# Loading the first chunks of wq in sets of every 4th or 2nd row, one row a descriptor

## The chip, the cores and the metric

The kernel runs on one core of a Trainium2 chip. The metric is the time of one execution on the device, in microseconds (us). The profile's span, from the first to the last instruction, is about 1.8 us shorter. The PE (TensorE) clock is granted in steps; the profile lists the granted share. Six runs of the kernel before on one chip lay within 0.3 us.

## The reference, cut to what matters

A decode step for one token: layer norm, attention over the last 4096 keys of 32 heads, output projection, and a gated MLP. Only the first product matters for the change.

```python
q = (x @ wq).reshape(B, Sq, Hq, Dh)          # x: 1 x 640, wq: 640 x 6144, bfloat16
k = k_cache[:, :, Sk - W:, :]                # 32 heads x 4096 keys x 192
v = v_cache[:, :, Sk - W:, :]
p = softmax(einsum(q, k) * Dh ** -0.5);  o = einsum(p, v)
h = x + o.reshape(1, 1, Hq * Dh) @ wo        # then the MLP on h
```

wq is 7.9 MB, k and v together 101 MB. Everything is read once.

## The kernel before

wq comes in five chunks of 128 rows by 6144 columns (1536 KB in the units of the profile). Two chunks share one large buffer. `load` puts one DMA on the queue of the sync engine (SP). The list of loads is `wq, k0, k1, k2, v0, ...`, and SP issues them in order, as far as buffers and semaphores allow.

```python
wq_v = A_wq.rearrange("(c p i) n -> c p (i n)", c=DC, i=4)   # 32 groups of 4 rows: 49152 contiguous bytes
...
def dma_wq(i):
    t = kvp.tile([P, KVE], BF16, tag="kv", name="wq_t")
    for c in range(2 * i, min(2 * i + 2, DC)):
        load(t[:, (c % 2) * HD:(c % 2 + 1) * HD], wq_v[c])   # one load: 128 partitions of 12288 bytes
    tiles[("wq", i)] = t
...
# q = x @ wq: six groups of matmuls; the first one takes chunk after chunk as it lands
for c in range(DC):
    for a in range(2):
        nc.tensor.matmul(psv, lhsT=xn2[:, c, a, :], rhs=wc[:, gq:gq + 4, a, w0:w0 + P], ...)
...
# the last v load, and the product with the last part of wo
nc.tensor.matmul(pv[p0:p0 + 2, 0:Dh], lhsT=E[:, j, :], rhs=vt[:, j * Dh:(j + 1) * Dh], ...)
nc.tensor.matmul(attn_ps[:, nb:nb + 1], lhsT=wo_t[:, ...], rhs=o[:, i:i + 1], ...)
```

The loads use eight semaphores in turn. The ninth load in flight has to wait until the first has landed. Three tiny loads from ScalarE's queue (x and two scalars) take part in the turn.

## Time and profile before

| | before |
|---|---|
| time, median (range) | 286.71 us (286.56 to 286.80, 6 runs) |
| span of the profiled run | 284.7 us |
| first load issued / first packets start | 0.74 / about 2.1 us |
| last wq chunk landed | 21.95 us |

From the page of the kernel before: span, busy time, the DMA row in 40 slices (tenths) with its GB/s, the load queue (packets, MB, share of 16 engines' span) and the shares of the chain that ended last.

```profile
span 284.7 us, 3101 instructions
PE 167.1 (59%) x1110; PEld 65.3 (23%) x1110; DVE 218.4 (77%) x288; ACT 75.2 (26%) x380; POOL 2.3 (1%) x10
...
DMA  8999999999998999999999999999999999999993
GB/s 332 435 435 408 435 429 402 444 463 435 435 435 382 435 442 443 427 464 424 414 442 421 443 428 439 407 457 428 410 435 456 442 442 383 435 435 425 401 406 141
...
q1 hardware_dynamic: 5384, 119.35, 97.8%
...
DMA 42%; DVE 41%; PE 13%; issue 2%; SPq 1%; ACT 0%; DVEq 0%; ACTq 0%
```

The load queue keeps 16 engines busy for 97.8% of the span. No compute engine comes near that. The chain's 41% for DVE is a trap: those links end in loads that already lie in a long queue (the k loads land 29.8 us after their issue, in the median).

The table of stretches shows it by stage. Its columns are the stretch, then busy time of PE, weight loads, DVE, ACT and POOL, the granted PE clock, the DMA share and GB/s.

```profile
core 0: us, PE busy (x) PEld busy (x) DVE busy (x) ACT busy (x) POOL busy (x), PEclk, DMA share, GB/s
2.00:22.00 20.00, 5.00 (x16) 1.78 (x17) 6.75 (x48) 0.22 (x2) 0.95 (x1) 1.00 1.03 433
220.00:274.00 54.00, 37.30 (x343) 16.36 (x342) 39.41 (x58) 6.72 (x24) 0.00 (x0) 0.90 0.99 421
```

A DMA share of 1.03 and 0.99, and 1.00 or 1.01 in the stretches between them: the stream is never empty until the tail. (A transfer is credited to the stretch in which it starts, so a share can pass 1.)

The timeline of the start shows SP's issues and the first matmuls of q. The columns are start, duration, engine, line, operation, operands, count, and in brackets the idle time before and what ended it.

```profile
0.74 3.15 SPq L58 DMA_DIRECT2D wq_t<-in_A_wq_dram  x5
...
9.76 1.03 PE L264 MATMUL sc_ps<-wq_t,xn_126 128*128 128x512 bf16 x2 [2.25 <-DVE xn_126 L251]
...
11.03 1.01 PE L264 MATMUL sc_ps<-wq_t,xn_126 128*128 128x512 bf16 x2 [0.24 <-DMA wq_t<-in_A_wq_dram]
...
14.70 1.01 PE L264 MATMUL sc_ps<-wq_t,xn_126 128*128 128x512 bf16 x2 [2.66 <-DMA wq_t<-in_A_wq_dram]
...
18.34 1.01 PE L264 MATMUL sc_ps<-wq_t,xn_126 128*128 128x512 bf16 x2 [2.63 <-DMA wq_t<-in_A_wq_dram]
...
21.95 2.29 PE L264 MATMUL sc_ps<-wq_t,xn_126 128*128 128x512 bf16 x5 [2.60 <-DMA wq_t<-in_A_wq_dram]
```

Each chunk lands about 3.65 us after the one before (11.03, 14.70, 18.34, 21.95). The first matmul at 9.76 waits for x, not for wq. So the landing of the last chunk tells how late the stream is.

Some readings need the packet records of the trace. Each holds start, duration, size and queue of one packet, but not its engine. A packet of 49152 B normally takes 1.815 us, one of 12288 B 0.460 us. Below, "excess" is what packets last beyond that, summed and divided by 16 engines. "Delay of the stream" is the mean end of the last 1024 packets of 49152 B (k and v), against the same packets of the kernel before.

### The profile page before, as it was taken

Reading aid. Unit: us, or ns where it says so; the run is one execution under the profiler, and the core shown is the slowest. Engines: PE = TensorE matmul, PEld = TensorE weight load, DVE = VectorE, ACT = ScalarE, POOL = GpSimd, SP = SyncE. Lnnn points to the kernel's source line nnn. Section 1 sums busy time; section 2 is a strip of 40 time slices with the busy share of each in tenths; the row PEclk is TensorE's granted clock in tenths of the full one; section 3 lists DMA queues with packets and bytes.
Section 4 is the critical chain, followed back from the end, with each engine's and each line's share of the span. In section 5 each row is a group of like instructions: output and inputs, shape, how many; then the busy total and the mean of one; then the engine's idle time right before and its main releaser. Section 6 shows DMA issues by size and latency. Waiting matters only on the chain.

```text
span 284.7 us, 3101 instructions
## 1 busy us (share of the span) xinstructions
PE 167.1 (59%) x1110; PEld 65.3 (23%) x1110; DVE 218.4 (77%) x288; ACT 75.2 (26%) x380; POOL 2.3 (1%) x10
## 2 busy tenths in 40 slices
PE   0329935773755377725852585536971767764774
PEld 0103412221211022211220121112320222321463
DVE  7300099889999999998499999996699949995443
ACT  2001247413274431122344440143101010202301
POOL 3000000000000000000000000000000000000000
PEclk9999979796598557955799558955797797999785
DMA  8999999999998999999999999999999999999993
GB/s 332 435 435 408 435 429 402 444 463 435 435 435 382 435 442 443 427 464 424 414 442 421 443 428 439 407 457 428 410 435 456 442 442 383 435 435 425 401 406 141
DMA packets 5404, 119.53 MB, mean 420 GB/s; under 512 B 973, under 2 KB 2254, under 8 KB 2830
## 3 DMA queue, kind: packets, MB, share of 16 engines
q1 hardware_dynamic: 5384, 119.35, 97.8%
q8 instruction: 8, 0.13, 0.2%
q14 instruction: 6, 0.05, 0.0%
q10 hardware_dynamic: 6, 0.00, 0.0%
HBM read 119.34 MB, written 0.00 MB: 419 GB/s over the span
## 4 chain that ended last, share of the span: by engine, by line
DMA 42%; DVE 41%; PE 13%; issue 2%; SPq 1%; ACT 0%; DVEq 0%; ACTq 0%
DVE k_t L316 22%; DMA k_t<-in_A_k_cache_dram 21%; DMA v_t<-in_A_v_cache_dram 9%; DMA wq_t<-in_A_wq_dram 7%; DMA wo_t<-in_A_wo_dram 5%; PE sc_ps L264 5%; DVE S L309 5%; DVE ob L437 4%; DVE S L330 4%; PE sc_ps L323 3%; PE pv_174 L412 1%; PE attn_ps L473 1%; SPq L58 1%; PE sm_ps L340 1%; DVE gm L342 1%
## 5 line engine op out<-in xcount | busy, mean ns | idle before, releaser
L316 DVE TENSOR_TENSOR k_t<-k_t,q_205 128x6144 bf16<-128x6144 bf16 x32 | 107.1, 3351 | 13.1 <-DMA k_t<-in_A_k_cache_dram 13.1
L323 PE MATMUL sc_ps<-k_t,ident_bf 128*128 128x512 bf16 x282 | 87.1, 468 | 50.6 <-DVE k_t L316 50.6
L306 ACT ACTIVATE k_t<-k_t 128x192 bf16<-128x192 bf16 x144 | 49.9, 347 | 32.8 <-DVE k_t L316 32.8
L323 PEld LDWEIGHTS <-ident_bf 128*128 128x128 bf16 x282 | 30.6, 113 | 98.3 <-issue 63.9
L306 ACT ACTIVATION_READ_ACCUMULATOR k_t<-k_t 128x1 f32 x144 | 26.8, 186 | 0.0
L309 DVE TENSOR_REDUCE S<-k_t 128x16 f32<-128x3072 bf16 x8 | 26.8, 3345 | 0.0
L264 PE MATMUL sc_ps<-wq_t,xn_126 128*128 128x512 bf16 x60 | 17.4, 449 | 10.4 <-DMA wq_t<-in_A_wq_dram 8.1
L330 DVE TENSOR_REDUCE S<-sc_ps 128x16 f32<-128x512 f32 (+1 forms) x32 | 21.8, 682 | 0.5 <-PE sc_ps L323 0.5
L273 DVE TENSOR_SCALAR sp_f<-sm_ps 128x1 f32<-128x1 f32 x3 | 0.3, 153 | 25.3 <-PE sm_ps L270 25.3
L359 ACT ACTIVATE E_125<-S,bias 128x64 bf16<-128x64 f32 x10 | 3.5, 360 | 48.1 <-DVE bias L349 48.1
L359 ACT ACTIVATE E_123<-S,bias 128x64 bf16<-128x64 f32 x12 | 4.2, 360 | 41.9 <-DVE bias L349 41.9
L359 ACT ACTIVATE E_124<-S,bias 128x64 bf16<-128x64 f32 x10 | 3.5, 361 | 37.9 <-DVE bias L349 37.9
L266 ACT ACTIVATE q_205<-sc_ps 128x512 bf16<-128x512 f32 x6 | 3.6, 597 | 30.1 <-PE sc_ps L264 30.1
L264 PEld LDWEIGHTS <-xn_126 128*128 128x128 bf16 x60 | 6.5, 109 | 20.9 <-issue 13.6
L412 PE MATMUL pv_174<-v_t,E_124 128*8 128x512 bf16 (+1 forms) x72 | 8.9, 521 | 2.0 <-DMA v_t<-in_A_v_cache_dram 2.0
L342 DVE TENSOR_REDUCE gm<-sm_ps 2x1 f32<-2x128 f32 x16 | 4.5, 278 | 7.1 <-PE sm_ps L340 7.1
L412 PE MATMUL pv_172<-v_t,E_125 128*8 128x512 bf16 (+1 forms) x72 | 7.5, 472 | 3.1 <-DMA v_t<-in_A_v_cache_dram 3.1
L412 PE MATMUL pv_174<-v_t,E_123 128*8 128x512 bf16 (+1 forms) x48 | 5.8, 521 | 1.0 <-DMA v_t<-in_A_v_cache_dram 1.0
L412 PE MATMUL pv_172<-v_t,E_123 128*8 128x512 bf16 (+1 forms) x72 | 6.2, 424 | 0.0
L412 PE MATMUL pv_174<-v_t,E_125 128*8 128x512 bf16 (+1 forms) x48 | 5.0, 474 | 1.6 <-DMA v_t<-in_A_v_cache_dram 1.6
L412 PEld LDWEIGHTS <-E_125 128*8 128x8 bf16 (+1 forms) x120 | 3.5, 87 | 9.3 <-issue 7.2
L412 PEld LDWEIGHTS <-E_124 128*8 128x8 bf16 (+1 forms) x120 | 3.6, 89 | 8.3 <-issue 6.4
(237 smaller groups left out, 148.3 us busy)
## 6 DMA issues: line engine op xcount, KB each, us to landing
k_t<-in_A_k_cache_dram SPq DMA_DIRECT2D x15, 3072.0 KB, 29.8
v_t<-in_A_v_cache_dram SPq DMA_DIRECT2D x15, 3072.0 KB, 29.6
wq_t<-in_A_wq_dram SPq DMA_DIRECT2D x5, 1536.0 KB, 11.2
wo_t<-in_A_wo_dram SPq DMA_DIRECT2D x7, 960.0 KB, 19.9
k_t<-in_A_k_cache_dram SPq DMA_DIRECT2D x2, 1536.0 KB
v_t<-in_A_v_cache_dram SPq DMA_DIRECT2D x1, 1536.0 KB
w_in_sb<-in_B_w_in_dram SPq DMA_DIRECT2D x2, 576.0 KB, 14.6
wo_t<-in_A_wo_dram SPq DMA_DIRECT2D x2, 480.0 KB, 13.8
```

What stands on the lines that cost most here:

```text
L58: eng.add_instruction(mybir.InstDMACopy(name=nc.get_next_instruction_name(), mode="Copy", queue="qSPDynamicHW", ins=eng.lower_ap_dma(in_, ...
L264: nc.tensor.matmul(psv, lhsT=xn2[:, c, a, :], rhs=wc[:, gq:gq + 4, a, w0:w0 + P], start=(c == 0 and a == 0), stop=(c == DC - 1 and a == 1))
L266: nc.scalar.activation(out=q2f[:, gq:gq + 4, w0:w0 + P], in_=psv, func=ACT.Copy, scale=scale / 16)
L306: nc.scalar.activation(out=k3[:, j, :], in_=k3[:, j, :], func=ACT.Copy, accum_out=S[:, j:j + 1])
L309: nc.vector.tensor_reduce(out=st[t]["S"][:, J - JS:J], in_=products(t)[:, J - JS:J, :], axis=AX.X, op=ALU.add)
L316: nc.vector.tensor_tensor(out=kc, in0=kc, in1=q2[:, t:t + 1, :].to_broadcast([P, JC, Dh]), op=ALU.mult)
L323: nc.tensor.matmul(psv, lhsT=ident_bf[:], rhs=products(t)[:, j0:j1, n * g:(n + 1) * g], start=(n == 0), stop=(n == Dh // g - 1))
L330: nc.vector.tensor_reduce(out=S[:, j0:j1], in_=st[t]["ps"][ch], axis=AX.X, op=ALU.add)
L342: nc.vector.tensor_reduce(out=gm[:], in_=mT[0:2, 0:P], axis=AX.X, op=ALU.max)
L359: nc.scalar.activation(out=E[:, :, a], in_=S[:], func=ACT.Exp, bias=bias[:, a:a + 1], accum_out=zq[q][:, a, b:b + 1])
L412: nc.tensor.matmul(pv[p0:p0 + 2 * n, :].rearrange("p (k r i) -> p k r i", k=n, r=32), lhsT=E[:, j0:j0 + n, :].rearrange("p j a -> p (j a)" ...
L437: nc.vector.tensor_reduce(out=ob[:, i0:i0 + ni], in_=flat.rearrange("p (k r i) -> p i r k", k=n, i=ni), axis=AX.X, op=ALU.add)
```

## The change

The intent, as far as the code tells it: smaller first loads with fewer descriptors, so that the stream starts sooner, each row on its own partition, in sets spread over all partitions. The first two chunks come in 4 sets of 32 rows, the next two in 2 sets of 64 rows, the last as before.

```diff
+    wq_rows = A_wq.rearrange("(c p) n -> c p n", c=DC)
+    WQ_PARTS = (4, 4, 2, 2, 1)
...
         for c in range(2 * i, min(2 * i + 2, DC)):
-            load(t[:, (c % 2) * HD:(c % 2 + 1) * HD], wq_v[c])
+            n = WQ_PARTS[c]
+            for j in range(n):
+                dst = t[j::n, (c % 2) * HD:(c % 2 + 1) * HD]
+                load(dst, wq_rows[c, j::n] if n > 1 else wq_v[c])
```

## The prediction

> **What bounds the kernel now.** The input stream. The page puts the load queue at 97.8% of 16 engines' span; the table of stretches shows a DMA share of 0.99 to 1.03 in every stretch from 2 to 274 us, while DVE has 77% and PE 59% of the span. By the packet records the 16 engines together lack only about 0.6 us of work between the first 5 us and the last 5. The chain of waits names DMA 42% and DVE 41%, but its DVE links end in loads that lie 14 to 30 us in the queue; a wait on DVE only shortens that backlog. Time = start of the stream + packet time per engine + about 10 us of tail after the last wo landing (274.0). The change can only act on the first two.
>
> **What it changes.** PE, DVE, ACT and POOL keep their instructions. On SP, four wq loads of 1536 KB become 4, 4, 2 and 2 loads, 13 in place of 5, the same bytes. Each of 16 engines moves such a chunk as 8 packets of 12288 B instead of 2 of 49152 B. The Trainium skill ("DMA: Bandwidth & Descriptors", Why a DMA increments its semaphore by 16 and not by 1) takes the largest count up to 16 that divides both slowest dimensions, so 32 and 64 rows still give 16 engines; the trace agrees for 32 source rows (2 packets on each engine). Eight more loads are a whole turn of the eight load semaphores, so later loads keep theirs.
>
> **Costs.** Packet records: 49152 B take 1.815 us, 12288 B (a late v load) 0.461. Four chunks: 32 x 0.461 - 8 x 1.815 = +0.23 us per engine. Eight more semaphore writes of about 0.01: at most +0.1. SP takes 0.55 to 0.63 us per load; a set of 32 rows lasts 0.92 on the engines, so SP keeps ahead. From the sixth load on SP waits for an earlier landing (reused semaphores), but with about 3.6 us of work queued, so I expect no hole.
>
> **Gains.** SP issues the first load at 0.74 us, packets start near 2.1, on five engines only at 2.7 to 2.9: 0.27 us idle per mean engine. The first 16 packets last on average 0.57 us more than 1.815. I read both as descriptors for 128 destination rows being made while engines wait; with 32 rows there are a quarter of them. At most 0.84 us (estimate) is to be had; I expect 0.65 of it.
>
> **On the critical path:** all of it, as the stream is never empty later: -0.65 + 0.3 = -0.35 us, 0.1%. Predicted 286.2 us, 8 in 10 within 285.5 to 286.8. Faster by over 2%: 0.005; within 2%: 0.985; slower by over 2%: 0.01.
>
> **What would show it right.** All engines start by about 2.2 us and the first packets last under 0.6 us; the wait for the last wq landing (21.95 us before, chain of waits) ends at 21.3 to 21.8; the last wo landing is earlier by as much; PE, DVE and ACT busy times stay; about 384 more data packets. The first wq matmul (9.76) waits for xn2, so PE starts no earlier.
>
> **What would make it wrong.** The 0.57 us is first access to memory and stays: then +0.1 to +0.3. A hole between sets because a short load is made slower than it is moved (DMA share below 1 in 3 to 8 us): up to +1. Strided single rows slower than 0.461. Or the queue runs dry later where I do not see it.

## The result

| | before | changed |
|---|---|---|
| time, median (range), 6 runs each | 286.71 us (286.56 to 286.80) | 288.25 us (287.92 to 289.31) |
| ratio, 95% interval | | 1.0059 (1.0041 to 1.0076) |
| span, profiled run | 284.7 | 286.8 |
| last wq chunk landed | 21.95 us | 22.90 us |
| delay of the stream | | 0.94 us |

A ratio is the mean time of one kernel's fast runs over that of the other's of the same rounds, so it is not quite the ratio of the medians. Executions over 1.5% slower than the fastest of the same kernel are left out of the means. The change is clear of noise, within 2%, and slower. It was predicted slightly faster, and the range (285.5 to 286.8) does not hold it.

The same lines of the page of the changed kernel, without the chain:

```profile
span 286.8 us, 3115 instructions
PE 169.8 (59%) x1110; PEld 66.2 (23%) x1110; DVE 218.2 (76%) x288; ACT 75.2 (26%) x380; POOL 2.3 (1%) x10
...
DMA  7999999999999999999999999999999999999991
GB/s 257 396 451 439 432 440 440 441 418 432 425 439 427 425 439 433 414 477 421 425 425 446 419 415 439 451 447 439 427 402 442 425 432 410 470 439 398 396 407 73
...
q1 hardware_dynamic: 5896, 119.35, 97.4%
```

PE, DVE and ACT do the same work. What differs is the first slice or two of the GB/s row: 257 and 396 instead of 332 and 435. The timeline of the start of the changed kernel:

```profile
0.74 8.46 SPq L58 DMA_DIRECT2D wq_t<-in_A_wq_dram  x13
...
9.75 1.04 PE L269 MATMUL sc_ps<-wq_t,xn_134 128*128 128x512 bf16 x2 [2.25 <-DVE xn_134 L256]
...
11.89 1.01 PE L269 MATMUL sc_ps<-wq_t,xn_134 128*128 128x512 bf16 x2 [1.10 <-DMA wq_t<-in_A_wq_dram]
...
19.26 1.03 PE L269 MATMUL sc_ps<-wq_t,xn_134 128*128 128x512 bf16 x2 [2.61 <-DMA wq_t<-in_A_wq_dram]
...
22.90 5.42 PE L269 MATMUL sc_ps<-wq_t,xn_134 128*128 128x512 bf16 x14 [2.60 <-DMA wq_t<-in_A_wq_dram]
```

The first matmuls that wait for a chunk, the second one, already come late (11.89 instead of 11.03). From then on the distance between chunks is about as before (19.26 to 22.90, 3.64 us), so nearly all of the loss is at the start. The last chunk is 0.95 us late.

The table of stretches for 5 to 12 us, first of the kernel before, then of the changed kernel:

```profile
core 0: us, PE busy (x) PEld busy (x) DVE busy (x) ACT busy (x) POOL busy (x), PEclk, DMA share, GB/s
5.00:8.00 3.00, 0.60 (x2) 0.50 (x2) 2.04 (x13) 0.00 (x0) 0.00 (x0) 1.00 0.69 295
8.00:12.00 4.00, 2.00 (x4) 0.53 (x5) 1.80 (x8) 0.00 (x0) 0.00 (x0) 1.00 1.14 492
...
5.00:8.00 3.00, 0.60 (x2) 0.50 (x2) 2.04 (x13) 0.00 (x0) 0.00 (x0) 1.00 0.93 369
8.00:12.00 4.00, 1.15 (x3) 0.34 (x4) 1.79 (x8) 0.00 (x0) 0.00 (x0) 1.00 0.98 396
```

In so short a stretch neither share nor rate tells the loss by itself: the kernel before has 0.69 and 295 between 5 and 8 us because its large packets are credited where they start. Their ratio does. A share of 1 would move 295 / 0.69 = 428 and 492 / 1.14 = 432 GB/s before, but 369 / 0.93 = 397 and 396 / 0.98 = 404 in the changed kernel: packets last longer than they should. The packet records say where. This is the sum for the first 24 us, in us a mean engine:

```
                                  before   changed
idle before all 16 engines run      0.27      0.15
excess of the first 16 packets      0.57      0.49
excess of later packets             0.04      0.71
idle between loads                  0.00      0.17
packets of wq by size (worked out)  0.00     +0.20
```

The 0.20 is 32 x 0.460 - 8 x 1.815. The sum of the differences is +0.84; eight more semaphore writes of 0.009 each bring it to +0.91. The k and v packets are 0.94 us late. The gain at the very start is there, but it is 0.2 us, not 0.65. The unforeseen part is 0.84 us: later packets that wait, and holes.

Loads landed at these times (mean over the engines, us): 3.65, 4.58, 5.80, 6.75, 7.78, 8.86, 9.87, 10.86 for the eight sets of 32 rows. The step should be 0.92 (two packets) and is 1.03 on average, (10.86 - 3.65) / 7, with the first slip at the third set. SP had issued it at 1.98 us, and the engines reached it at about 4.6, when the second set had landed.

The remaining 0.6 us of the time (1.54 less 0.94) lies in the tail. That is taken up under "the tail" below.

### The profile page after: what moved, and what is told of

The parts are those of the page before. It is cut to its first block, busy times and chain, and to the rows that moved or that the text cites. A ratio compares the mean times of both kernels' runs of the same rounds, so it can differ in the third digit from the quotient of the medians.

```text
span 286.8 us, 3115 instructions
## 1 busy us (share of the span) xinstructions
PE 169.8 (59%) x1110; PEld 66.2 (23%) x1110; DVE 218.2 (76%) x288; ACT 75.2 (26%) x380; POOL 2.3 (1%) x10
## 4 chain that ended last, share of the span: by engine, by line
DVE 39%; DMA 37%; PE 17%; issue 3%; SPq 1%; ACT 0%; DVEq 0%
DVE k_t L321 22%; DMA k_t<-in_A_k_cache_dram 21%; DMA v_t<-in_A_v_cache_dram 9%; DMA wq_t<-in_A_wq_dram 7%; DVE ob L442 5%; PE sc_ps L269 5%; DVE S L335 4%; PE sc_ps L328 4%; DVE S L314 3%; PE attn_ps L478 2%; PE pv_182 L417 2%; PE sm_ps L345 1%; SPq L58 1%; PE pv_182 L407 1%; DVE gm L347 1%
## 5 line engine op out<-in xcount | busy, mean ns | idle before, releaser
L328 PE MATMUL sc_ps<-k_t,ident_bf 128*128 128x512 bf16 x282 | 88.8, 474 | 50.7 <-DVE k_t L321 50.6
```

Of the source, the lines that this page charges most:

```text
L328: nc.tensor.matmul(psv, lhsT=ident_bf[:], rhs=products(t)[:, j0:j1, n * g:(n + 1) * g], start=(n == 0), stop=(n == Dh // g - 1))
```

## The experiments

Times and ratios are against runs of the kernel before in the same rounds on the same chip. Delays and landings are against its one trace, which is of an earlier round. The theories:

- T1: short loads at the start are made ready too late, and engines reach them before they can move.
- T2: one-row packets are slow at the start.
- T3: waits for reused semaphores.
- T4: only SP's issue time.
- T5: the tail at half clock.
- T6: a fixed cost of each load on the engines.
- T7: two engines share one way into SBUF, when a set of rows reaches only some of the ways.
- T8: a load has to be issued some time before the engines reach it.

Diffs are against the changed kernel unless said otherwise.

### One-row packets alone

```diff
-    WQ_PARTS = (4, 4, 2, 2, 1)
+    WQ_PARTS = (1, 1, 1, 1, 1)
-                load(dst, wq_rows[c, j::n] if n > 1 else wq_v[c])
+                load(dst, wq_rows[c, j::n] if c < 4 else wq_v[c])
```

> Five loads as before, but chunks 0 to 3 with one row a descriptor (12288 B packets). T1 (an engine reaches the descriptors of the next short load before they are ready, while the queue is nearly empty): only the packet cost of +0.23 us, the last wq landing (21.95 before, 22.90 in the changed kernel) at 22.0 to 22.3, time +0.2 to +0.4 us against before. T2 (one-row packets are themselves slower while the stream starts, however many loads they come in): last wq landing at 22.7 to 23.1, time +1.0 to +1.6 us, as in the changed kernel. T3 (waits for reused semaphores on the queue's sequencer): no such wait here, so as T1.

Measured: 286.65 us, ratio 0.9998 (0.9981 to 1.0016). The stream is 0.19 us late, as the packet size costs. The line of the timeline where the last chunk of wq has landed:

```profile
21.93 2.29 PE L269 MATMUL sc_ps<-wq_t,xn 128*128 128x512 bf16 x5 [2.57 <-DMA wq_t<-in_A_wq_dram]
```

T2 falls. Packets of one row cost the stream their 0.2 us and nothing else. What loses must come with cutting the chunks into several loads.

### Two sets for each chunk

```diff
+    WQ_PARTS = (2, 2, 2, 2, 1)
```

> Sets of 2, 2, 2, 2, one row a descriptor: 9 loads. T1: half the boundaries of short loads, so between the two: last wq landing near 22.4, time +0.4 to +0.9 us. T2: as the changed kernel, 22.7 to 23.1 and +1.0 to +1.6 us. T3: one wait on a landing (the sixth load) against five in the changed kernel, so at most +0.4 us.

Measured: 287.16 us, ratio 1.0022 (1.0003 to 1.0042); delay 0.28 us, last wq landing 22.29. Between the two, as T1 has it, nearer to no loss. The first of its six runs, the profiled one, took 289.02 us and the other five 287.1 to 287.4. The stream of that trace is no later than 0.3 us, so the other 1.8 us of that run are not the stream's. Its clock record shows half clock from 266.3 us to the end (see the tail).

### Only the first chunk in four sets

```diff
+    WQ_PARTS = (4, 1, 1, 1, 1)
```

> Only chunk 0 in four sets, the other chunks as before (8 loads). T1: the stall of the third set (0.28 us a mean engine in the changed kernel) stays, the later ones go; start spread 0.4 instead of 0.8 us gains 0.1: last wq landing 22.1 to 22.4, time +0.2 to +0.6 us. T2: only 8 one-row packets an engine, a quarter of the loss: +0.2 to +0.5 us. T3: three loads wait for semaphores, nearly all long free: about +0.1 us.

Measured: 287.70 us, ratio 1.0038 (1.0022 to 1.0054); delay 0.65 us. The line of the timeline where the last chunk of wq has landed:

```profile
22.48 1.87 PE L269 MATMUL sc_ps<-wq_t,xn 128*128 128x512 bf16 x4 [2.63 <-DMA wq_t<-in_A_wq_dram]
```

Four short loads do most of what eight do. The landing at 22.48 is just past T1's range, and the time, +0.9 us in the median, is above what all three theories expected: a miss. The third and fourth set waited, and neither waits for a semaphore, so T3 does not explain them. The fifth load waited too (its first packets lasted 0.18 us longer in the mean), though it is a whole chunk and was issued 3.8 us before the engines reached it. So the load that waits need not be short itself.

### Only the last chunk in four sets, twice

```diff
+    WQ_PARTS = (1, 1, 1, 1, 4)
```

> Only chunk 4 (the last) in four sets, when four long loads are already queued ahead. T1 and T2 (both speak of the start of the stream only): only the packet cost of +0.06 us; last wq landing 21.9 to 22.1, time within 0.2 us of before. If short strided loads or one-row packets cost something at any time: last wq landing 22.2 or later, +0.3 us or more.

> Only chunk 4 in four sets, once more: its loads were only 0.17 us later than before, but its time was +0.9 us in the median with a wide scatter (286.8 to 288.7), which no theory of the start explains. T5: the last wq landing is again 21.9 to 22.1, and the runs that are slow have the half clock in the tail (matmuls of the last v load over 4.5 us); the median may then fall anywhere from +0.1 to +1.2. If something else costs: the landing of the last wo load is 0.5 us or more later than before.

Measured: 287.66 us (286.79 to 288.70), ratio 1.0029; again: 286.89 us (286.61 to 287.93), ratio 1.0013 (0.9991 to 1.0036). Delays 0.09 and 0.31 us; in both the sets landed every 0.92 us and no packet of them waited. So the same short loads are free behind a full queue. The time of the first was a miss (expected within 0.2 us, got +0.9), which the stream does not explain. See the tail.

### The first chunk in eight sets

```diff
+    WQ_PARTS = (8, 1, 1, 1, 1)
```

> Chunk 0 in eight sets of 16 rows: one packet of 0.46 us an engine and load. T1, sharpened by the runs so far (each load, however small, needs about 1.2 us before its packets are ready, so short loads at the start are ready more slowly than they are moved): the first chunk lands about 8 x 1.2 + 2.7 = 12 us (7.3 before), last wq landing 25 to 27 us, time +3.5 to +5 us. T4 (only the sequencer's 0.62 us per issue limits): first chunk at 8 to 8.5, last wq landing 22.8 to 23.3, time +1 to +1.5 us. If a load's cost goes with its rows: no more than the changed kernel, +1 us or less.

Measured: 289.73 us, ratio 1.0094; delay 3.16 us, last wq landing 24.86. Sets of 16 rows, 0.46 us of packets, landed about every 0.9 us while SP issued one every 0.63. I read this as T1 with 0.9 instead of 1.2 us a load. That reading did not last.

### Sets behind one whole chunk

```diff
+    WQ_PARTS = (1, 4, 4, 2, 1)
```

> Chunk 0 whole as before, then the sets 4, 4, 2 and chunk 3 in 2: the same number of short loads as in the changed kernel, but behind 3.6 us of queued work. T1: the queue hides their making; only the packet cost of +0.2 us stays: last wq landing 22.0 to 22.3, time +0.1 to +0.5 us. If short loads cost wherever they stand in the first 20 us: last wq landing 22.6 or later and +0.9 us or more, as in the changed kernel.

Measured: 288.13 us, ratio 1.0038 (1.0026 to 1.0050); delay 1.29 us, the last wq landing at 23.20. A miss for T1 as it stood. The line of the timeline where the last chunk of wq has landed:

```profile
23.20 5.28 PE L269 MATMUL sc_ps<-wq_t,xn 128*128 128x512 bf16 x12 [2.60 <-DMA wq_t<-in_A_wq_dram]
```

The first four sets landed every 0.92 to 0.94 us, nearly without waiting. But the sixth load, held by a reused semaphore until the whole first chunk had landed, was issued at 7.7 us, and the engines reached it at about 10.5. From 10 to 14 us packets again had 0.57 us of excess and engines 0.21 us of idle time.

### A late start by itself

Diff against the kernel before:

```diff
+    dummy = const.tile([1, 16], BF16)
+    for k_ in range(2):
+        load(dummy[:, 8 * k_:8 * k_ + 8], A_wo[0:1, 8 * k_:8 * k_ + 8])
     issue()
```

> The kernel before with two loads of 16 bytes (one engine) ahead of the wq loads: the stream starts two issue times, 1.2 to 1.3 us, later and nothing else changes. If a late start goes one for one into the time: last wq landing 23.1 to 23.3, time +1.1 to +1.4 us. If the tail adds to any delay through the granted clock of TensorE: +1.5 us or more. If the stream has slack: less than +1.

Measured: 288.27 us (288.08 to 289.62), ratio 1.0055 (1.0037 to 1.0072); delay 1.56 us. The line of the timeline where the last chunk of wq has landed, above the 23.1 to 23.3 expected:

```profile
23.55 4.85 PE L267 MATMUL sc_ps<-wq_t,xn 128*128 128x512 bf16 x11 [2.60 <-DMA wq_t<-in_A_wq_dram]
```

The median is 1.31 us up, the mean 1.6, and the span of this trace 1.7 (286.4 against 284.7). A late stream goes about one for one into the time. No slack shows later.

### Without the tiny loads in between, and with fewer waits

```diff
-    nc.scalar.dma_start(out=wsp_bf[:, 0:1], in_=B_w_sp[0:1])      # and b_sp
...
             nc.scalar.activation(out=q2f[:, gq:gq + 4, w0:w0 + P], in_=psv, func=ACT.Copy, scale=scale / 16)
+            if gq == 0 and w0 == 0:
+                nc.scalar.dma_start(out=wsp_bf[:, 0:1], in_=B_w_sp[0:1])      # and b_sp
```

> The changed kernel with the two tiny loads of wsp moved from 1.5 us to about 24 us: they no longer lie between the first short loads, and seven instead of five loads are issued before SP waits for a landing. T1: no great change, last wq landing 22.6 to 23.1, time +0.9 to +1.6 us against before. T3 (semaphore waits) or contention of the tiny loads with the third set: the stall of the third set goes, last wq landing 22.3 to 22.5, time +0.4 to +0.7 us.

Measured: 288.35 us, ratio 1.0060 (1.0027 to 1.0093); delay 0.95 us, last wq landing 23.32, later than any theory expected. No gain. In the changed kernel neither the tiny loads nor the semaphore waits (five loads before the first wait there, seven here) are the cause. T3 falls for it; in the run with the sets behind one whole chunk such a wait did matter.

### Two queues

```diff
+    WQ_PARTS = (8, 1, 1, 1, 1)
-                load(dst, wq_rows[c, j::n] if n > 1 else wq_v[c])
+                if n > 1 and j % 2 == 1:
+                    nc.scalar.dma_start(out=dst, in_=wq_rows[c, j::n])
+                else:
+                    load(dst, wq_rows[c, j::n] if n > 1 else wq_v[c])
...
+    nc.scalar.dma_start(out=x_row[:], in_=A_x[0])                 # moved up, ahead of the sets
     issue()
```

> The kernel with chunk 0 in eight sets of 16 rows (one landing about every 0.9 us, last wq landing 24.86, +2.8 us), with every second set issued from ScalarE's queue instead of SP's. If the 0.9 us a load belongs to one issuing queue: sets land about every 0.5 us, last wq landing 22.3 to 23.0, time +0.4 to +1.2 us. If both queues share what makes the packets of a load ready: landing stays about every 0.9 us, last wq landing 24.5 to 25.2, time +2.4 to +3.2 us.

Measured: 290.11 us, ratio 1.0117; last wq landing 24.79, delay 3.11 us, as with one queue. The Trainium skill says so ("DMA: Bandwidth & Descriptors", Issuing engines are not separate DMA queues): all queues run on the same 16 engines, and a second one saves only issue time. The landing, 24.79 against 24.86, does not contradict it, but this run is a poor test: sets of 16 rows turned out to be slow for another reason, on any queue (see the last chunk in eight sets).

### Adjacent rows

```diff
+                m = P // n
-                dst = t[j::n, ...]
+                dst = t[j * m:(j + 1) * m, ...]
-                load(dst, wq_rows[c, j::n] if n > 1 else wq_v[c])
+                load(dst, wq_rows[c, j * m:(j + 1) * m] if n > 1 else wq_v[c])
```

> The changed kernel with sets of 32 or 64 adjacent rows and partitions instead of every 4th or 2nd. If spreading a set over all partitions matters (fewer ways into SBUF for 32 adjacent partitions): packets of 12288 B take clearly longer than 0.46 us, last wq landing over 25 us, time +3 us or more. If it does not: as the changed kernel, last wq landing 22.7 to 23.2, time +1.2 to +1.8 us.

Measured: 301.40 and 301.41 us, ratio 1.0513; two more runs, the profiled one among them, were at 324 and 325 and are not explained. Two chunks in the timeline of that trace:

```profile
25.40 1.03 PE L270 MATMUL sc_ps<-wq_t,xn 128*128 128x512 bf16 x2 [6.32 <-DMA wq_t<-in_A_wq_dram]
32.70 1.04 PE L270 MATMUL sc_ps<-wq_t,xn 128*128 128x512 bf16 x2 [6.27 <-DMA wq_t<-in_A_wq_dram]
```

A chunk takes 7.3 us instead of 3.65, packets 0.92 instead of 0.46. Four chunks at +3.65 make +14.6 us, which is about what the fast runs show (301.4 less 286.5). The Trainium skill ("SBUF — State Buffer", Door 1: The DMA port swizzle) states that DMA bandwidth depends on how many of the 16 SBUF ports the partitions reach, that bits 2 to 4 and bit 6 of the partition number choose the port, and that partitions 0 to 31 or 0 to 63 reach only 8. This run agrees: half the rate. So the spread over the partitions in the change is needed, if the chunk is cut by rows at all.

### The last chunk in eight sets

```diff
+    WQ_PARTS = (1, 1, 1, 1, 8)
```

> Chunk 4 (the last) in eight sets of 16 rows, behind four whole chunks; 0.46 us of packets an engine and set. T1 (a short load's packets are made ready at most about every 0.9 us, which a full queue hides): the sets land about every 0.46 us, all within 3.7 us, last wq landing 21.9 to 22.3, time -0.1 to +0.6 us (the tail's scatter). T6 (each load keeps the engines at least about 0.9 us, queue or no queue): the sets land every 0.9 us, last wq landing 25 us or later, time +2.5 us or more. The eighth set is issued only when chunk 3 has landed (reused semaphore) and may come late by up to 0.5 us under both.

Measured: 291.80 us, ratio 1.0189; delay 4.37 us. T1 as an account of the 0.9 us falls: a full queue hides nothing. The stretch from 16 to 22 us:

```profile
core 0: us, PE busy (x) PEld busy (x) DVE busy (x) ACT busy (x) POOL busy (x), PEclk, DMA share, GB/s
16.00:22.00 6.00, 1.01 (x2) 0.11 (x1) 0.00 (x0) 0.00 (x0) 0.00 (x0) 1.00 0.93 234
```

The engines are busy for 0.93 and move 234 GB/s. Packets take 0.85 to 0.96 us instead of 0.46. By the port map of the same page, rows j, j+8, j+16, ... have bit 2 in common and reach 8 of 16 ports. So the eight-set runs show a different effect from the changed kernel's, and it remained to separate T6 from T7.

### The last chunk in eight column parts

```diff
+    WQ_PARTS = (1, 1, 1, 1, 8)
-                dst = t[j::n, (c % 2) * HD:(c % 2 + 1) * HD]
-                load(dst, wq_rows[c, j::n] if n > 1 else wq_v[c])
+                w = HD // n
+                dst = t[:, (c % 2) * HD + j * w:(c % 2) * HD + (j + 1) * w]
+                load(dst, wq_rows[c, :, j * w:(j + 1) * w] if n > 1 else wq_v[c])
```

> Chunk 4 in eight loads of all 128 rows and an eighth of the columns: as many loads, of as many bytes, at the same place as in the run with eight sets of 16 rows behind four whole chunks (landings every 0.92 us, last wq landing 26.93, +5 us). Eight packets of 1536 B an engine and load, 0.065 us each. T6 (each load keeps the engines about 0.9 us): landings every 0.9 us, last wq landing 25 us or later, time +2.5 us or more. T7[...]: landings every 0.52 to 0.65 us, last wq landing 22.4 to 23.3, time +0.5 to +1.5 us.

The stretch from 16 to 22 us of this run:

```profile
core 0: us, PE busy (x) PEld busy (x) DVE busy (x) ACT busy (x) POOL busy (x), PEclk, DMA share, GB/s
16.00:22.00 6.00, 2.34 (x6) 0.54 (x5) 0.00 (x0) 0.17 (x1) 0.00 (x0) 1.00 0.95 363
```

As many loads of as many bytes, over all partitions: 363 GB/s instead of 234, landings about every 0.5 us, nearly all packets at their 0.065 us. T6 falls: a load as such costs the engines nothing behind a full queue. The time, 289.04 us (ratio 1.0076), was a miss: +2.2 us where +0.5 to +1.5 was expected. Delay 1.17: 0.53 us from the packet size, 0.4 us because the first packets at 2 us were late by chance of this run, and the rest at the first k load behind the parts.

### The last chunk in sets at stride 7

```diff
+    WQ_PARTS = (1, 1, 1, 1, 8)
+                rows = slice(0, P) if n == 1 else slice(j, 112, 7) if j < 7 else slice(112, P)
+                load(t[rows, ...], wq_v[c] if n == 1 else wq_rows[c, rows])
```

> Chunk 4 in eight sets of 16 rows as in the run at stride 8 (landings every 0.92 us, packets 0.85 to 0.96 us), but seven of the sets take every 7th row of rows 0 to 111, and the eighth rows 112 to 127. T7: [...]median packet of the seven sets 0.46 to 0.55 us, mean below 0.65, and the eighth set[...] about four times 0.46 us. T6: packets and landings as at stride 8, 0.9 us for all sets.

Measured: 290.79 us, ratio 1.0138; delay 3.86 us. The seven sets landed about every 0.67 us instead of 0.92. Their packets: 0.46 for half of the first set, then 0.57 to 0.82 (median about 0.66). The eighth set, on 4 ports by the same map, took 0.78 to 1.53. The direction is T7's, the size is not: 0.46 to 0.55 was expected. With the stride alone changed, the packets' time changed, so ports matter; that they are all of it at 16 rows is not shown.

### The first chunk in four column parts

The column edit above with:

```diff
+    WQ_PARTS = (4, 1, 1, 1, 1)
```

> Chunk 0 in four loads of all 128 rows and a quarter of the columns, the others whole: as many loads of as many bytes as in the run with chunk 0 in four sets of 32 rows (loads 0.71 us later than before, last wq landing 22.48, time +0.9 to +1.1). 3072 B packets of about 0.12 us cost +0.24 us by themselves. T7 (two engines in turn on the same ways into SBUF with sets of every 4th row; not with 128 rows): mean delay of the loads 0.2 to 0.4 us, no packets of the second to fourth load much above 0.12 us, last wq landing 22.0 to 22.3, time +0.2 to +0.6 us. T1 or T6 (short loads as such): mean delay 0.7 us or more, stalls at the third load, last wq landing 22.4 or later.

Measured: 288.14 us, ratio 1.0045 (1.0018 to 1.0073); delay 0.74 us. The line of the timeline where the last chunk of wq has landed:

```profile
23.14 14.13 PE L270 MATMUL sc_ps<-wq_t,xn 128*128 128x512 bf16 x52 [2.63 <-DMA wq_t<-in_A_wq_dram]
```

This is the run that decides for the changed kernel. All partitions take part, so by T7 nothing should be lost, and the loss is about the same: 0.74 less 0.24 for the packets is 0.50; with four sets of 32 rows it was 0.65 less 0.06, which is 0.59. Packets again waited at the first of the third and fourth load. T7 is not the cause in the changed kernel. Short loads at the start are, with nothing long queued ahead of them.

### Sets behind two whole chunks

```diff
+    WQ_PARTS = (1, 1, 4, 4, 1)
```

> Chunks 0 and 1 whole, then chunks 2 and 3 in four sets each of every 4th row: eight short loads, as in the changed kernel. T8 (a load must be issued about 3 to 4 us before the engines reach it; the sets behind one whole chunk lost 1.36 us because the sixth load, held by a reused semaphore, was issued only 2.8 us ahead): here every set is issued 4 us or more ahead, so only the packet cost of +0.12 us: no idle engines between 5 and 20 us, mean delay of the loads 0.05 to 0.3 us, last wq landing 21.9 to 22.4, time 0 to +0.7 us (with the tail's scatter). If sets of every 4th row cost wherever they stand (two engines in turn on the same ways into SBUF): mean delay 0.7 us or more.

Measured: 287.41 us (287.18 to 288.66), ratio 1.0035 (1.0019 to 1.0051), a little above the range; delay 0.29 us. The line of the timeline where the last chunk of wq has landed:

```profile
22.28 2.29 PE L269 MATMUL sc_ps<-wq_t,xn 128*128 128x512 bf16 x5 [2.56 <-DMA wq_t<-in_A_wq_dram]
```

Eight sets of every 4th row, landed every 0.92 us; no packet of them waits (excess 0.01 us) and no engine is idle after the start. The 0.29 us are no more than packet size (0.12) and the start of this run (0.23: more idle time, less excess) account for. The sixth load, held by the reused semaphore just as in the run behind one whole chunk, was issued at 7.6 us, but the engines reached it only at about 13.2. So the same sets cost 0.84 us at the front and nothing here.

This speaks for T8's direction, not for a fixed lead of 3 to 4 us. In the changed kernel's two traces the second set was reached only 2.2 to 2.3 us after its issue and lost 0.01 us at most, the third, reached 2.6 us after its issue, lost about 0.3, and the ninth, reached 4.9 us and more after its issue, still lost 0.12 and 0.09. No single lead time fits these.

### The changed kernel again, and the tail

> The changed kernel once more, for a second trace. T1: last wq landing again 22.7 to 23.2 (21.95 before), mean delay of the loads 0.8 to 1.1 us, kept to the end; time +1.2 to +1.7 us. T5 (what exceeds the delay of the loads comes from the tail, where TensorE runs at half clock): in a run with a span above 286.5 the matmuls of the last v load take over 4.5 us (3.9 before) and the project step ends after the last wo landing by more than before; in a run near 286.1 they take 3.5 to 4.2 us.

Measured: 288.27 us (287.72 to 289.44), ratio 1.0060 (1.0034 to 1.0087); last wq landing 22.68, delay 0.84 us. The stream part repeats. For the tail, these are the matmuls of the last v load (the largest block of them) and the last projection, first in the kernel before:

```profile
268.55 0.98 PE L402 MATMUL pv_174<-v_t,E_123 128*2 128x192 bf16 x28
...
274.08 0.53 PE L478 MATMUL attn_ps<-o_1888,wo_t 128*128 128x1 bf16 x15 [0.30 <-DMA wo_t<-in_A_wo_dram]
```

28 matmuls in 0.98 us; the second half of the projection waits for the last wo load, so the stream still decides. In the changed kernel's first trace:

```profile
270.24 2.44 PE L407 MATMUL pv_182<-v_t,E_131 128*2 128x192 bf16 x44
...
275.49 0.89 PE L483 MATMUL attn_ps<-o_1896,wo_t 128*128 128x1 bf16 x30 [0.32 <-DVE o_1896 L469]
```

44 matmuls in 2.44 us, and no wait for a load before the projection: PE is late. The clock record shows half clock from 266.4 to 273.2 us. And in the second run with only the last chunk in four sets:

```profile
269.64 2.44 PE L407 MATMUL pv<-v_t,E 128*2 128x192 bf16 x44
```

Here the last wo load landed 0.4 us later than before, but the span is 286.2, 1.5 us more; the other three runs of that kernel have spans of 284.9 to 285.2. From these I estimate that half clock in the tail costs about 1 us (1.5 less 0.4) in the runs where it falls on these matmuls, whatever the loads did. The other traces fit. In four of the 18 fast traces at least 3.6 us of the whole block of last-v matmuls ran at half clock (the changed kernel's first, two sets for each chunk, the first chunk in eight sets, this one). There the block took 4.7 to 5.3 us, and the span less the delay of the stream is 285.8 to 286.7 us. In the other 14 at most 2.3 us ran at half clock, the block took 3.5 to 4.1 us, and the span less the delay is 284.7 to 285.4. The repeated changed kernel, with the profiled span at 285.9, took 3.7 us for the whole block of last-v matmuls (before 3.9, changed kernel's first trace 4.7), and its span is 1.2 us above before: mostly stream. The Trainium skill ("TensorE: Matmul & The Clock Gate", Part 1) has the clock at half as the default and released by activity; these traces agree that the share is 0.5 or 1 and changes in steps of 3.4 us. Why it falls on the tail in more of the changed kernel's runs than in the kernel before, whose runs stay within 0.3 us on the first chip (286.29 to 288.30 over all later ones), is open. No run here moved the clock alone.

## Why the prediction was wrong

- **What bounds the kernel**: right. The stream is the time, and two dummy loads in front show a delay going through about one for one.
- **16 engines for 32 and 64 rows**: right. The trace has 512 packets of 12288 B for the four chunks, 32 an engine.
- **Packet cost +0.23 us**: right. With one-row packets in five loads the stream was 0.19 us late.
- **"I expect 0.65 of it"** (the gain at the start): wrong in size. Idle time and first-packet excess fell from 0.84 to 0.64 us, a gain of 0.20. The excess of the first packets, 0.57, stayed at 0.49. Over the fast traces the two together are 0.84 to 1.11 us in the ten whose first load has 128 rows in packets of 12288 B or more, and 0.60 to 0.77 in the four whose first load is a set of 32 rows: about 0.3 us gained, under half of 0.65. So the making of descriptors for 128 rows was at most a part of it; the prediction named "first access to memory" as the alternative, and no run here shows which part of it that is.
- **"SP keeps ahead" and "so I expect no hole"**: this is the step that failed. SP does keep ahead: it issues every 0.62 us what takes 0.92 us to move. The queued work was there as well: the sixth load was reached 3.6 us after its issue, as predicted. But issued is not ready. From the third load on, the packets did not run at full rate when the engines reached them, which cost 0.84 us (0.67 of longer packets, 0.17 of holes) where nothing was expected. The prediction did name such a hole, up to +1 us, among what would make it wrong. The runs show that this is a matter of short loads with nothing queued ahead: 0.50 us with column parts, 0.59 with four sets, none behind two whole chunks. What inside the path from issue to packet takes the time was not found.
- **"DMA share below 1 in 3 to 8 us"** as the sign of a hole: a poor sign. Between 5 and 8 us the share was 0.93 in the changed kernel, but 0.69 in the kernel before, which had no hole there.
- **The tail** was not in the sum. Half clock on the last matmuls adds about 1 us in some runs, by the estimate above.

The changed kernel is slower by 0.9 us of stream, shown, and by about 0.6 us of tail, seen in one of its two traces and argued for the rest. That the clock makes the tail longer goes by comparing traces; no run set the clock. No version here beat the kernel before; one-row packets in five loads equal it.

## What to carry to other kernels

In a kernel bound by its input stream, put large loads first and cut loads finely only behind a queue that is several microseconds long (here two whole chunks, about 7 us, were enough); queued work has to hide the making ready of the loads behind it, and reused semaphores can shorten that queue. How much lead a load needs was not settled here. When a set of rows is cut out of a tile, count how many SBUF ports its partitions reach before timing it. A busy DMA engine is no proof of a full rate: read the GB/s for each unit of share, or the packets' durations, and not the share alone.

## What the Trainium skill lacked or had wrong

- "DMA: Bandwidth & Descriptors" gives about 0.6 us to the first byte for loads from SP or ACT. Here the first packets started 1.34 us after the first issue began and 0.8 us after it ended, and the first packets then lasted longer than later ones, by 0.57 us (49152 B, kernel before) and 0.49 us (12288 B, changed kernel).
- The same page has a fixed cost for each transfer, fitted on loads from GpSimd, and asks for loads of 1 MiB or more. It does not say that a long queue can hide that cost: sets of 384 KB landed every 1.03 us at the start (0.92 would be full rate) and every 0.92 us behind two whole chunks.
- No page says how long before its use a load must be issued. In these traces packets waited at loads reached 2.6 to 4.9 us after their issue, and not at the one reached 5.6 us after it (behind two whole chunks); but the second set of the changed kernel, reached 2.3 us after its issue, did not wait either. So the lead is not one number.
- "SBUF — State Buffer" has the port map, but speaks of ranges of partitions. Strided sets seem to fall under it too, though the times at stride 7 were longer than T7 expected: 16 rows at stride 8 took 0.85 to 0.96 us a packet, at stride 7 mostly 0.57 to 0.82, where 0.46 is usual; 32 rows at stride 4 took 0.46.
